# A two-branch layer on one core: merged table products, three more kinds of buffers, fewer idle products and a new written-out order

## The chip, the cores and the metric

The kernel runs on one core of a Trainium2 chip. A core has five engines that this document names as the profile does: PE (matrix products, with PEld for its weight loads), DVE (vector), ACT (scalar, with activation functions), POOL and SP (which here only issues transfers). The metric is the device time of one execution in microseconds (us).

## The reference

The input x has 2048 tokens of 512 channels. It is normalised (mean and variance over the channels), and two branches of the normalised xn are added to x:

```python
xn = _layernorm(x)
# A: a long convolution along the tokens, one kernel of 2048 lags per channel
P = exp(dt * A * l)                         # 512 channels x 128 complex modes x 2048 lags
K = real(sum over modes of C * P * dt * B)  # 512 x 2048
yA = irfft(rfft(xn, 4096) * rfft(K, 4096))[:2048] + xn * Dskip
# B: a gated unit
yB = (sigmoid(xn @ w_gate) * (xn @ w_up)) @ w_down    # 512 -> 1792 -> 512
out = x + yA + yB
```

Inputs and output are bf16.

## The kernel before

**Branch B** works in four groups of 512 tokens. For a group it takes the 1792 inner channels as 14 tiles of 128, two tiles at a time: a gate projection (four products of 128x512 into one PSUM bank, L1082), a sigmoid on ACT (L1098), an up projection (four products, L1107) and a product h on DVE (L1129). The table `UPS` gives each of the 28 pairs of tiles a mode: whether ACT first copies the up projection from PSUM to SBUF (L1118) and whether DVE multiplies both tiles in one instruction. In modes 2 and 3 DVE reads a wide SBUF copy, in 4 and 5 one half of it comes from PSUM, in 6 two SBUF halves, in 0 two PSUM halves, in 1 one wide PSUM operand. `GATES` lists pairs whose two sigmoids are one instruction. Then four down projections follow for the group, 14 products each (L1160).

**Branch A** replaces the Fourier transform of 4096 by two stages of products with small constant matrices. Stage one (L710, eight steps `fx2`) transforms xn along 32 rows; its result goes to DRAM (`z_scr`) and is loaded again in another layout. For each of two channel halves there are eight units, worked on two at a time, so eight pairs in all. For each pair come the forward product of the pair (L914, `fm`), the spectrum of the kernel from the lag table kT with a constant block E that is loaded for each unit (L930, `fk`), and the complex products of both on DVE (L935, L939). The inverse product of the pair follows (`mv_`). It exists in three forms, chosen by the table `SUMS`: with 0 the products go to PE as they are (L963); with 1 DVE first adds them once (L946, L947, `fsum`) and PE has fewer columns to stream (L975); with 2 DVE adds twice (L949 too) and PE has fewer still. The result goes to DRAM (`v_scr`) and comes back for the last stage (L1039, `s2_mm`), which is added to branch B's output: for the first three token groups by DVE (L1053) into a buffer, for the last group in PSUM, with DVE adding x at the end (L1180).

**The lag table.** K is built from powers of exp(dt A). A chain of 12 squarings in f32 (ACT L682, DVE L691 and L693) gives the powers W, which POOL casts to bf16 by a transfer (L687). From W the tables G and H are built for each of four channel chunks by complex products on DVE (`cmul`): two products of all of `lo` with the real and with the imaginary part of a power (L748, L749) and then a difference and a sum (L753, L754). There are ten such products in each chunk, with n = 1, 1, 2, 2, 4, 4, 4, 4, 7 and 8; one product has 256 n elements in each partition. PE contracts G and H over the modes (L833, `f_k`), a selection follows (L862), and kT is complete.

**What sets the order.** Every step is entered in a list (`pl.add`) with an engine and its dependences, and numbered in the order of entry. The list `ORDER` gives the sequence in which steps are issued; each engine works through its own steps in that sequence, waiting where a dependence is not met. SP's transfers are such a queue too: a transfer that waits holds up those behind it. Buffers come from pools of slots (`es` for E, `kb` for the kernel's spectrum, `vs` for results on their way to `v_scr`, `zx` for what comes back from `z_scr`); a slot is taken by `acq` and given back by `rel` as `ORDER` is read. `ON_DVE` lists, by number, copies and normalisations that go to DVE and not to ACT; `ON_ACT` lists the token tiles whose mean and variance ACT computes (L556 to L558) and not DVE (L561, L565, L566). Before the first data have arrived PE runs idle products of zeros (L541, `keep_warm`): one step of 9, and four steps whose lengths are in `WARM`.

Of the kernel before, what the change touches and what calls it, by code (L numbers as in the profile page):

```python
# [11 lines left out]
F32 = mybir.dt.float32  # L12
# [37 lines left out]
SUMS = ((0, 0, 0, 2), (1, 0, 1, 2))  # L50
WARM = (2, 2, 2, 2)
# [132 lines left out]
def _consts():  # L184
# [26 lines left out]
ORDER = [  # L211
# [131 lines left out]
def kernel(  # L343
# [83 lines left out]
    s1, mn = (at(OFF["pq"], [2, 64])[:, n, :] for n in range(2))  # L427
    s2 = at(OFF["tmp"], [2, 64])
    rr = at(OFF["tmp"] + KB // 2, [D])
    W = [at(OFF["W%d" % p], [12, 2, DW]) for p in range(NP)]  # L430
    gc = at(OFF["gc"], [2, D])
    xn = at(OFF["xn"], [NT, D])

# [245 lines left out]
    for k in range(12):  # L679
# [5 lines left out]
        def f_cw(cur=cur, k=k):  # L685
            for p in range(NP):
                P.dma_start(out=W[p][:, k], in_=cur[:, p])  # L687
# [570 lines left out]
```

## Time and profile before

| | |
|---|---|
| three runs | 213.96, 215.98 and 218.8 us; median 215.98 us |
| the profiled execution | 214.29 us, span 212.6 us |
| busy, share of the span | PE 202.3 us (95%), DVE 194.7 us (92%), ACT 171.3 us (81%), POOL 31.7 us (15%) |
| busy time of weight loads | 104.2 us (49%) |
| granted clock of PE | 0.999 |
| transfers | 42.37 MB, mean 199 GB/s |

The span goes from the first to the last instruction of the profiled execution. A row of the groups gives line, engine, operation, output and inputs with partitions x elements, the count, then busy time and the mean duration of one in ns, and then the engine's idle time just before such instructions with what ended it. "Big" is the name of the one large SBUF tile in which most buffers lie, "banks" is PSUM.

### The profile page before, as it was taken

The numbers are of one execution on the slowest core, as the hardware profiler recorded it, in microseconds if no ns is written. First come the engines' busy times: TensorE is split into PE (matmuls) and PEld (weight loads), VectorE is DVE, ScalarE is ACT, GpSimd is POOL, SyncE is SP. The second block draws the span as 40 slices with busy tenths as digits, with TensorE's granted clock in tenths as the row PEclk, the third lists the DMA queues.
The fourth block names the chain that finished last, engine by engine and source line by source line (L and its number), as shares of the span: only waits on it lengthen the run. The fifth ranks groups of instructions, "written<-read, shape, count | busy, mean of one in ns | idle before, by whom it ended". The sixth has DMA issues, their size and how long they took to land.

```text
span 212.6 us, 5668 instructions
## 1 busy us (share of the span) xinstructions
PE 202.3 (95%) x2263; PEld 104.2 (49%) x2291; DVE 194.7 (92%) x410; ACT 171.3 (81%) x272; POOL 31.7 (15%) x67
## 2 busy tenths in 40 slices
PE   7899999999999999999999999999999998999990
PEld 2664444444444354445556365446446554544570
DVE  3899999999999999999999999999999999892792
ACT  3899999999999997868989999949388997971000
POOL 4302316343240000004400000000010060000000
PEclk9999999999999999999999999999999999999999
DMA  6999999958976072594885333425765599989956
GB/s 193 380 417 366 311 243 215 199 112 192 193 129 171 18 233 100 152 266 130 150 263 165 108 92 100 142 99 166 213 204 105 171 294 221 338 241 267 204 186 224
DMA packets 44045, 42.37 MB, mean 199 GB/s; under 512 B 8809, under 2 KB 37746, under 8 KB 44018
## 3 DMA queue, kind: packets, MB, share of 16 engines
q1 hardware_dynamic: 39074, 36.95, 55.8%
q0 software_dynamic: 4512, 4.73, 14.2%
q8 instruction: 18, 0.29, 0.6%
q10 hardware_dynamic: 432, 0.33, 0.5%
q14 instruction: 9, 0.07, 0.1%
HBM read 25.21 MB, written 12.07 MB: 175 GB/s over the span
## 4 chain that ended last, share of the span: by engine, by line
PE 77%; ACT 13%; DMA 3%; DVE 2%; issue 2%; POOL 0%; SPq 0%; DVEq 0%; ACTq 0%; POOLq 0%
PE banks L1160 21%; PE banks L1107 17%; PE banks L1082 17%; PE banks L930 7%; ACT hT_sb L1098 3%; DMA v_scr<-big 3%; PE banks L541 3%; PE banks L833 3%; PE banks L963 2%; PE banks L914 2%; ACT big L297 2%; PE banks L862 1%; ACT big L682 1%; PE banks L975 1%; PE banks L710 1%
## 5 line engine op out<-in xcount | busy, mean ns | idle before, releaser
L297 ACT ACTIVATE big<-banks 128x1024 bf16<-128x1024 f32 (+4 forms) x78 | 71.2, 957 | 6.5 <-PE banks L963 2.2
L1082 PE MATMUL banks<-xnT,wg_sb 128*128 128x512 bf16 (+1 forms) x233 | 53.0, 361 | 1.2 <-ACT xnT L297 0.6
L1107 PE MATMUL banks<-xnT,wu_sb 128*128 128x512 bf16 x212 | 52.7, 380 | 0.8 <-issue 0.3
L1160 PE MATMUL banks<-wd_sb,hT_sb 128*128 128x512 bf16 (+1 forms) x233 | 50.1, 366 | 0.3 <-issue 0.2
L1160 PEld LDWEIGHTS <-hT_sb 128*128 128x128 bf16 x238 | 22.8, 98 | 25.2 <-issue 1.2
L1098 ACT ACTIVATE hT_sb<-banks 128x512 bf16<-128x512 f32 x56 | 32.4, 630 | 3.3 <-PE banks L1082 2.9
L1082 PEld LDWEIGHTS <-wg_sb 128*128 128x128 bf16 x244 | 22.8, 98 | 24.7 <-issue 3.9
L1107 PEld LDWEIGHTS <-wu_sb 128*128 128x128 bf16 x224 | 20.9, 98 | 25.6 <-issue 2.8
L748 DVE TENSOR_TENSOR big<-big 128x1024 bf16<-128x1024 bf16 (+4 forms) x40 | 26.8, 671 | 0.4
L749 DVE TENSOR_TENSOR big<-big 128x1024 bf16<-128x1024 bf16 (+4 forms) x40 | 26.7, 667 | 0.0
L1118 ACT ACTIVATE big<-banks 128x512 bf16<-128x512 f32 (+1 forms) x39 | 25.2, 677 | 0.6 <-PE banks L1107 0.5
L935 DVE TENSOR_TENSOR big<-big 128x2048 bf16<-128x2048 bf16 x16 | 19.4, 1222 | 1.0 <-ACT big L297 1.0
L930 PE MATMUL banks<-big 128*128 128x256 bf16 x160 | 20.1, 273 | 0.0
L930 PEld LDWEIGHTS <-big 128*128 128x128 bf16 x160 | 15.3, 98 | 5.4 <-issue 1.2
L802 ACT ACTIVATE sq_sb<-big 128x256 bf16<-128x256 bf16 (+2 forms) x20 | 13.4, 688 | 5.3 <-DVE big L754 4.1
L687 POOL DMA_DIRECT2D big<-big x24 | 13.0, 546 | 28.7 <-DVE big L693 19.7
L753 DVE TENSOR_TENSOR big<-big 128x512 bf16<-128x512 bf16 (+4 forms) x40 | 16.7, 417 | 0.2
L754 DVE TENSOR_TENSOR big<-big 128x512 bf16<-128x512 bf16 (+4 forms) x40 | 16.6, 415 | 0.0
L1129 DVE TENSOR_TENSOR hT_sb<-hT_sb,big 128x1024 bf16<-128x1024 bf16 (+1 forms) x29 | 16.0, 559 | 0.3 <-ACT big L1118 0.2
L682 ACT ACTIVATE big<-big 128x1024 f32<-128x1024 f32 x11 | 11.8, 1076 | 0.1
L561 DVE BATCH_NORM_STATS2 stats<-big 128x6 f32<-128x512 bf16 x12 | 8.3, 688 | 3.4 <-DMA big<-in_A_u_dram 3.4
L939 DVE TENSOR_TENSOR big<-big 128x1024 bf16<-128x1024 bf16 x16 | 11.0, 688 | 0.0
(101 smaller groups left out, 208.0 us busy)
## 6 DMA issues: line engine op xcount, KB each, us to landing
big<-c_E SPq DMA_DIRECT2D x16, 320.0 KB, 4.0
z_scr<-big SPq DMA_DIRECT2D x16, 256.0 KB, 2.8
big<-z_scr SPq DMA_DIRECT2D x16, 256.0 KB, 4.2
v_scr<-big SPq DMA_DIRECT2D x16, 256.0 KB, 3.3
big<-big POOLq DMA_DIRECT2D x24, 128.0 KB, 3.5
big<-in_A_u_dram SPq DMA_DIRECT2D x4, 512.0 KB, 7.8
big<-v_scr SPq DMA_DIRECT2D x4, 512.0 KB, 6.3
wu_sb<-in_B_w_up_dram SPq DMA_DIRECT2D x2, 896.0 KB, 10.4
```

The lines of the kernel that those rows point to most:

```text
L297: nc.scalar.activation(out=a, in_=b, func=ACT.Identity)
L748: V.tensor_tensor(out=wide(outp), in0=wide(lo), in1=mre, op=ALU.mult)
L749: V.tensor_tensor(out=wide(tb()), in0=wide(lo), in1=mim, op=ALU.mult)
L753: V.tensor_tensor(out=outp[:, :, 0], in0=outp[:, :, 0], in1=tb()[:, :, 1], op=opr)
L754: V.tensor_tensor(out=outp[:, :, 1], in0=outp[:, :, 1], in1=tb()[:, :, 0], op=opi)
L930: T.matmul(bank(sk[kt == NKT - 1])[:, DW * c:DW * c + DW], es()[:, c, kt, :], kT[p][:, kt, :], start=kt in (0, NKT - 1), stop=kt >= NKT - 2)
L935: V.tensor_tensor(out=pp()[:, :, 0:4, :], in0=xx()[:, :, 0, :].unsqueeze(2).to_broadcast([128, 2, 4, DW]), in1=kb().unsqueeze(1).to_broadc ...
L1082: T.matmul(bank(sl)[:, c0:c1], w_at(w, CUT_G, kt, k), xnT[:, grp, kt, c0:c1], start=(kt == 0), stop=(kt == KT - 1))
L1098: S.activation(out=o_, in_=i_, func=ACT.Sigmoid)
L1107: T.matmul(bank(sl), w_at(wu_sb, CUT_U, kt, k), xnT[:, grp, kt, :], start=(kt == 0), stop=(kt == KT - 1))
L1118: S.activation(out=o_, in_=i_, func=ACT.Identity)
L1160: T.matmul(bank(po)[:, 0:c[1] - c[0]], hT_sb[:, hts[k // 2].idx, k % 2, jj * 128:(jj + 1) * 128], wd_sb[:, k, c[0]:c[1]], start=first and ...
```

## The change

- In `cmul` the two products with the real and the imaginary part become one of twice the size where both results fit the temporary buffer of 2048 elements (n = 1, 2 and 4); the difference and the sum then read both from there. For this W is kept with real and imaginary part of a chunk side by side, the f32 powers too, and the first power is made by one product instead of two.
- `es` has six slots where it had three, `kb` three where it had two, `vs` three where it had two. The added ones lie in places that are free only later: those of `es` and `kb` after the lag tables are done, that of `vs` after the first forward product.
- `keep_warm` runs 8 idle products in its first step instead of 9, and 0, 2, 0, 2 in the others instead of 2, 2, 2, 2.
- For token tiles 4 to 15 epsilon is added to the variances once for four tiles and no longer once for each tile.
- `SUMS`, `UPS`, `GATES`, `ON_DVE` and `ON_ACT` have new entries. In `SUMS`, by the diff, the entry 0 stands twice (before: four times), 1 twice (twice) and 2 four times (twice).
- `ORDER` is a new list. The added epsilon steps move the numbers of later steps by up to three. Some numbers, before and after: the last stage-one product 154 and 132; the first forward product 338 and 341, with its two loads from `z_scr` 336, 337 and 340, 339; the second forward product 360 and 363; the last inverse product 507 and 510; the last two stores to `v_scr` 509, 511 and 512, 514. In the new list, on SP, 131 is the load that transposes the last token group, 350 the first load of E, and 169, 134, 171 and 136 are the last stores to `z_scr`.

```diff
-SUMS = ((0, 0, 0, 2), (1, 0, 1, 2))
-WARM = (2, 2, 2, 2)
+SUMS = ((0, 1, 0, 2), (1, 2, 2, 2))
+WARM = (0, 2, 0, 2)
...
-UPS = (5, 3, 5, 0, 3, 5, 2, 2, 1, 3, 5, 2, 2, 3, 3, 5, 2, 6, 2, 6, 3, 6, 2, 5, 2, 4, 2, 4)
-GATES = ()
-ON_DVE = (41, 99, 100, 101, 102, 111, 112, 126, 180, 181, 263, 293, 422, 442, 785, 787, 795)
-ON_ACT = (3, 7, 13, 15)
+UPS = (4, 5, 0, 0, 3, 3, 1, 2, 6, 2, 2, 5, 4, 5, 6, 2, 2, 2, 2, 6, 6, 3, 4, 2, 0, 2, 5, 0)
+GATES = (2, 6, 25)
+ON_DVE = (100, 101, 103, 115, 127, 183, 184, 214)
+ON_ACT = (2, 7, 8, 9, 14)
 ORDER = [
...
+    237, 238, 239, 233, 213, 167, 168, 698, 130, 240, 241, 131, 707, 242, 245, 169, 256, 234, 243, 246, 244, 170, 247,
+    132, 133, 257, 135, 709, 747, 350, 248, 258, 249, 251, 775, 259, 710, 737, 777, 708, 134, 776, 749, 264, 250, 265,
+    260, 267, 268, 732, 781, 171, 252, 266, 261, 269, 727, 270, 728, 296, 262, 739, 734, 748, 783, 253, 779, 136, 729,
+    272, 730, 271, 409, 273, 340, 276, 339, 341, 343, 263, 277, 778, 254, 344, 349, 342, 351, 361, 362, 735, 736, 751,
+    278, 365, 274, 780, 279, 345, 346, 275, 352, 347, 807, 785, 750, 363, 753, 809, 372, 808, 364, 366, 384, 373, 280,
...
+    491, 831, 822, 833, 859, 858, 832, 842, 844, 509, 490, 824, 860, 835, 501, 502, 470, 510, 492, 527, 826, 701, 865,
+    846, 872, 834, 836, 511, 512, 513, 514, 530, 531, 874, 876, 862, 864, 528, 855, 856, 866, 880, 883, 712, 802, 524,
+    702, 878, 881, 713, 612, 803, 804, 884, 525, 792, 613, 703, 893, 882, 521, 887, 805, 522, 714, 622, 793, 794, 704,
...
-    W = [at(OFF["W%d" % p], [12, 2, DW]) for p in range(NP)]
+    W = [at(OFF["W%d" % p], [12, 2, 2, CW]) for p in range(NP)]
...
-    warm = [keep_warm(9, -10)]
+    warm = [keep_warm(8, -10)]
...
+        if i1 > LN_ACT:
+            st = [pl.add("DVE", 0.08, lambda: V.tensor_scalar(out=ln_ve[:, i0:i1], in0=mv[:, i0:i1, 1], scalar1=EPS, scalar2=None, op0=ALU.add), st, prio)]
...
     def f_w0():
-        wd = lambda n: pt_[n].rearrange("p (w d) -> p w d", w=NP)
-        V.tensor_tensor(out=wt[0][:, :, 0], in0=wd("rr"), in1=wd("sh"), op=ALU.mult)
-        V.tensor_tensor(out=wt[0][:, :, 1], in0=wd("rr"), in1=wd("sn"), op=ALU.mult)
+        cs = at(pt0_sh, [2, D], F32).rearrange("p c (w d) -> p w c d", w=2 * NP)
+        V.tensor_tensor(out=wt[0], in0=pt_["rr"].rearrange("p (w d) -> p w d", w=2 * NP).unsqueeze(2).to_broadcast([128, 2 * NP, 2, CW]), in1=cs, op=ALU.mult)
...
     def cmul(lo, outp, n, m, conj, buf, deps, prio):
...
+        fit = 2 * ne <= 2048
+        flat = lambda v: v.rearrange("p r c k h -> p (r c) (k h)")
...
         def f_a():
-            V.tensor_tensor(out=wide(outp), in0=wide(lo), in1=mre, op=ALU.mult)
-            V.tensor_tensor(out=wide(tb()), in0=wide(lo), in1=mim, op=ALU.mult)
+            if fit:
+                V.tensor_tensor(out=tb()[:, 0:2 * ne], in0=flat(lo).unsqueeze(1).to_broadcast([128, 2, 2 * NPR, 2 * n]),
+                                in1=m.rearrange("p m (r h) -> p (m r) h", h=2).unsqueeze(2).to_broadcast([128, 2 * NPR, 2 * n, 2]), op=ALU.mult)
+                return
+            for i, o_ in enumerate((flat(outp), tb()[:, 0:ne])):
+                V.tensor_tensor(out=o_, in0=flat(lo), in1=m[:, i, :].rearrange("p (r h) -> p r h", h=2).unsqueeze(2).to_broadcast([128, NPR, 2 * n, 2]), op=ALU.mult)
...
-    kgen[3][0].rel += tuple(_Slot(k, i) for k, n, m in (("pp", 2, 3), ("zx", 2, 10)) for i in range(n, m))
+    kgen[3][0].rel += tuple(_Slot(k, i) for k, n, m in (("pp", 2, 3), ("zx", 2, 10), ("es", 3, 6)) for i in range(n, m))
+    kq_free[0].rel += (_Slot("kb", 2),)
...
-                es=[OFF["W0"], OFF["W0"] + 2560, OFF["W0"] + 5120], kb=[OFF["W0"] + 7680, OFF["W0"] + 9728],
-                vs=[OFF["xn"] + 14 * KB, OFF["lad"] + 10 * KB],
+                es=[OFF["W0"], OFF["W0"] + 2560, OFF["W0"] + 5120, OFF["lad"] + 12 * KB, OFF["tmp"] + 3 * KB // 2, None],
+                kb=[OFF["W0"] + 7680, OFF["W0"] + 9728, KQ], vs=[OFF["xn"] + 14 * KB, OFF["lad"] + 10 * KB, OFF["kx"] + 6 * KB],
...
+        if not v_st[0]:
+            mm.rel += (_Slot("vs", 2),)
```

More of the change, by code (lines that the diff above doesn't have):

```diff
@@ L557, in fa1 @@
                     S.activation(out=glu_sb[:, 7, :], in_=xn[:, i, :], func=ACT.Square, scale=-1.0, bias=mv[:, i, 0:1], accum_out=mv[:, i, 1:2])
-                    S.activation(out=ln_ve[:, i:i + 1], in_=mv[:, i, 1:2], func=ACT.Identity, scale=1.0 / D, bias=eps[:])
+                    if i < LN_ACT:
+                        S.activation(out=ln_ve[:, i:i + 1], in_=mv[:, i, 1:2], func=ACT.Identity, scale=1.0 / D, bias=eps[:])
+                    else:
+                        S.activation(out=mv[:, i, 1:2], in_=mv[:, i, 1:2], func=ACT.Identity, scale=1.0 / D)
             else:
@@ L565, in fa2 @@
                     V.bn_aggr(out=mv[:, i, :], in_=stats[:, i % 4, :])
-                    V.tensor_scalar(out=ln_ve[:, i:i + 1], in0=mv[:, i, 1:2], scalar1=EPS, scalar2=None, op0=ALU.add)
+                    if i < LN_ACT:
+                        V.tensor_scalar(out=ln_ve[:, i:i + 1], in0=mv[:, i, 1:2], scalar1=EPS, scalar2=None, op0=ALU.add)
             if i < LN_ACT:
@@ L618, in ptile @@
         return t
-    names = ["dtb", "z_re", "z_im", "w0", "rn", "rr", "sn", "sh"]
+    names = ["dtb", "z_re", "z_im", "w0", "rn", "rr", "sh", "sn"]
     pt_ = {n: ptile(BF if n == "dtb" else F32) for n in names}
+    pt0_sh = pt0[0] - 4 * KB
     pt0[0] = OFF["lad"] + 12 * KB
@@ L686, in f_cw @@
             for p in range(NP):
-                P.dma_start(out=W[p][:, k], in_=cur[:, p])
+                P.dma_start(out=W[p][:, k], in_=cur[:, 2 * p:2 * p + 2])
         c_op = pl.add("POOL", 1.0, f_cw, [cur_op], PLAD + k * 0.01 + 0.005, dma=(512 * KB, _rate(1024), 1.0))
@@ L774 @@
             for q in range(0, n, st):
-                last = cmul(G[:, :, :, q:q + st, :], G[:, :, :, n + q:n + q + st, :], st, W[c // 2][:, 4 + lev, :, ws],
+                last = cmul(G[:, :, :, q:q + st, :], G[:, :, :, n + q:n + q + st, :], st, W[c // 2][:, 4 + lev, c % 2],
                             True, "tg", [last, W_op[4 + lev]], PC)
@@ L896, in slot, with view @@
         sl = _Slot(pool)
-        return sl, lambda: at(HOME[pool][sl.idx], shape)
+        def view():
+            off = HOME[pool][sl.idx]
+            if off is not None:
+                return at(off, shape)
+            v = sq_sb[:].rearrange("p a b -> p (a b)")[:, 0:int(np.prod(shape))]
+            return v.rearrange("p (a b c) -> p a b c", a=shape[0], b=shape[1])
+        return sl, view
     v_st, z_free = [[] for _ in VPART], []
```

21 lines of the change are left out of this document (10 added, 11 removed), and 69 rows, old and new, of the table ORDER.

## The prediction

> **What bounds the kernel now.** I read the page's busy shares first, then the busy time of each engine in stretches, then the chain of waits.
>
> ```profile
> PE 202.3 (95%) x2263; PEld 104.2 (49%) x2291; DVE 194.7 (92%) x410; ACT 171.3 (81%) x272; POOL 31.7 (15%) x67
> ```
> ```profile
> 15.00:190.00 175.00, 171.96 (x2058) 86.52 (x2081) 171.96 (x363) 158.25 (x252) 27.27 (x49) 1.00 0.69 186
> ```
>
> The second row is the stretch from 15 to 190 us: 175 us, then the busy time of PE, of PE's weight loads, of DVE, ACT and POOL, and the granted clock, 1.00. PE and DVE are both busy for 171.96 us of it, 98%; ACT for 90%. So two engines bind at once, with 3.0 us idle each, and a change has to shorten both queues to move the end. That PE's busy time is real work shows in the chain of waits (start, us, what):
>
> ```profile
> 1.38 5.73 PE banks L541 x13
> ...
> 84.14 0.35 PE banks L710 x8
> 84.49 0.79 PE banks L862 x64
> ...
> 89.76 6.04 PE banks L1160 x28
> ...
> 96.59 1.42 PE banks L833 x123
> ...
> 126.30 1.44 PE banks L963 x64
> ...
> 183.61 0.79 PE banks L975 x32
> ...
> 189.69 0.57 PE banks L975 x16
> ```
>
> The 28 down products take 6.04 us, 0.216 us each with nothing between them; a group of four (one gate or up projection) is then 0.86 us and a group of 14 is 3.02.
>
> The Trainium skill, Perfetto Trace Analysis, Identifying the Most-Contended Engine, says that matmul busy time is a bad measure and weight-load share a better one. By that page PE, with 49% of weight loads, would have room and DVE alone would bind; the 0.216 us spacing of the 28 speaks against it. What would follow is the first rival.
>
> The profiled execution took 214.29 us, 1.7 over its span of 212.6. The three runs go from 213.96 to 218.8 with a median of 215.98, 0.8% above the profiled one. I sum against the span and scale at the end.
>
> **PE's part.** An inverse product of a pair costs 1.44 us without sums (L963), 0.79 after one step, 0.57 after two (both L975). By the diff two pairs leave the first kind, one to 0.79 and one to 0.57, and one goes from 0.79 to 0.57: 2.88 - 0.79 - 0.57 + 0.22 = 1.74 us less. The diff's table shows four pairs with two steps, not five; I cost four. Five idle products go: one of the 13 at the start (5.73 / 13 = 0.44 us each) and the two later pairs, of which the rows show the second:
>
> ```profile
> 28.62 0.60 PE L541 MATMUL banks<-glu_sb 128*128 128x512 bf16 x2
> ```
>
> At 0.216 us each these four are 0.86 us, in a queue with no room. PE: 1.74 + 0.86 + 0.44 = 3.0 us less. The first transposes stand right behind the idle products, so nothing takes that place.
>
> **DVE's part.** Groups, with busy time, then mean ns of one:
>
> ```profile
> L748 DVE TENSOR_TENSOR big<-big 128x256 bf16<-128x256 bf16 x8 | 3.0, 380 | 0.0
> L748 DVE TENSOR_TENSOR big<-big 128x512 bf16<-128x512 bf16 x8 | 3.5, 436 | 0.1
> L748 DVE TENSOR_TENSOR big<-big 128x1024 bf16<-128x1024 bf16 x16 | 11.1, 691 | 0.3
> L748 DVE TENSOR_TENSOR big<-big 128x2048 bf16<-128x2048 bf16 x4 | 4.9, 1222 | 0.0
> L946 DVE TENSOR_TENSOR big<-big 128x768 bf16<-128x768 bf16 x8 | 4.4, 553 | 0.0
> L949 DVE TENSOR_TENSOR big<-big 128x512 bf16<-128x512 bf16 x4 | 1.7, 425 | 0.1
> L561 DVE BATCH_NORM_STATS2 stats<-big 128x6 f32<-128x512 bf16 x12 | 8.3, 688 | 3.4 <-DMA big<-in_A_u_dram 3.4
> L566 DVE TENSOR_SCALAR ln_ve<-mv 128x1 f32<-128x1 f32 x12 | 1.8, 154 | 0.4
> L582 DVE TENSOR_SCALAR big<-big,mv,ln_ri 128x512 bf16<-128x512 bf16 x11 | 4.3, 414 | 0.2 <-POOL ln_ri L516 0.2
> L292 DVE CAST big<-banks 128x1024 bf16<-128x1024 f32 x2 | 2.4, 1220 | 0.0
> L292 DVE CAST big<-banks 128x512 bf16<-128x512 f32 x3 | 2.0, 691 | 0.0
> L1129 DVE TENSOR_TENSOR hT_sb<-hT_sb,big 128x1024 bf16<-128x1024 bf16 x15 | 10.2, 688 | 0.0
> L1129 DVE TENSOR_TENSOR hT_sb<-hT_sb,banks 128x512 bf16<-128x512 bf16 x10 | 6.7, 682 | 0.4 <-PE banks L1107 0.4
> L1129 DVE TENSOR_TENSOR hT_sb<-hT_sb,big 128x512 bf16<-128x512 bf16 x14 | 5.8, 420 | 0.3 <-ACT big L1118 0.2
> ```
> ```profile
> 168.23 0.55 DVE L946 TENSOR_TENSOR big<-big 128x768 bf16<-128x768 bf16 x1
> 168.70 0.55 DVE L947 TENSOR_TENSOR big<-big 128x768 bf16<-128x768 bf16 x1
> ```
>
> Neighbours overlap: the second row starts 0.47 us after the first, which lasts 0.55. So an instruction occupies DVE for its duration less 0.08 us.
>
> - **Merged products**, two of a size (L748 and its twin L749) into one of twice the size: 8 x (2 x 0.30 - 0.36) + 8 x (2 x 0.36 - 0.61) + 16 x (2 x 0.61 - 1.14) = 1.9 + 0.9 + 1.3 = 4.1 us less. The smallest kind costs more per element than the others; if its merged form keeps that, its 1.9 is nothing and the term is 2.2.
> - **Layernorm**: one statistics tile goes to ACT (0.61 and its aggregate 0.1), six 128x1 additions go (0.07 each): 1.2 less. Two normalisations go to ACT: 0.7 less.
> - **Copies**: ten on DVE become three. Two of 1.14, three of 0.61 and two small ones at about 0.35 go: 4.8 less.
> - **Sums**: four units more get a first step (two of 0.47) and four more a second (0.34): 5.1 more.
> - **GLU products**: counting the table of modes, 15 wide ones (0.61) become 12, 8 half-and-half (0.34 + 0.60) become 7, 3 of two SBUF halves (0.68) become 4, 1 of two PSUM halves (1.20) becomes 4: 1.5 more.
>
> DVE: -4.1 - 1.2 - 0.7 - 4.8 + 5.1 + 1.5 = -4.2 us. ACT takes what DVE gives away, 6.7 us at DVE's own durations: with it 158.25 becomes 165 of 175, 94%, still the third. The wide layout of W and the single product at w0 move the same elements; I cost them at nothing, hidden by the table chain's own waits on DVE. More buffers for E, kb and vs take away waits of ACT; one of those stopped PE, and I let it pay for waits that the new order brings:
>
> ```profile
> 180.07 0.62 PE L914 MATMUL banks<-big,m 64*32 64x512 bf16 x15 [0.96 <-ACT big L297]
> ```
>
> **The order, and the tail.** In the new list one up group more (0.86 us) stands behind the last inverse product, and seven h products of DVE in place of four (1.8 us). Ahead of that product PE thus has 3.9 us less and DVE 6.0 less. PE gives the smaller: 189.69 - 3.9 = 185.8 us. Behind it lie now:
>
> ```profile
> 191.41 1.34 SPq L448 DMA_DIRECT2D v_scr<-big  x2
> 192.80 4.83 SPq L448 DMA_DIRECT2D big<-v_scr  x7
> ```
> ```profile
> L448 SPq DMA_DIRECT2D big<-v_scr x5: 302/415/421, 195.5 to 197.2; - x5
> ...
> DMA to landing us min/median/max: 5.8/6.2/6.6
> ```
> ```profile
> 201.75 1.93 PE L1039 MATMUL banks<-big 128*64 128x256 bf16 x26
> ...
> 205.81 1.70 PE L1160 MATMUL banks<-wd_sb,hT_sb 128*128 128x256 bf16 x14
> ```
>
> The product ends at 190.26; ACT copies, SP has stored by 192.75, and only when that has landed, at 195.5, do the last loads leave; they land 5.8 to 6.2 us later, at 201.3 to 201.7. The product that needs them runs at 201.75: 11.5 us of other PE work covered a chain of 11.0 to 11.4. In the new list the cover is two up groups (1.72), two down groups (6.04) and three output products (4 matmuls each; the 26 above in 1.9 us make that 0.25): 8.5 us. If the chain stays at 11.4, PE waits 2.9 us; if the loads take 3 us, as the store did, the chain is 8.2 and PE waits for nothing. I take 1.5, the middle, because in the new list fewer large loads leave just ahead of the last.
>
> The Trainium skill, DMA: Bandwidth & Descriptors, section on queues, rings and completion order, says that an engine consumes descriptors in ring order, so a load waits for bytes issued ahead of it. By it the loads above were slow because of the large ones just ahead, and the wait would be near 0: 1.5 us less than my sum. No row of before has a last load alone.
>
> PE's end: before, 189.69 to 207.51 is 17.8 us; now 17.8 + 0.86 + 1.5 after 185.8 gives 206.0. From PE's end to the span's end were 5.1 us, of which 0.4 because the last addition stood behind others; the new list puts only its own two there: 4.7. Span 206.0 + 4.7 = 210.7, execution 212.4, 0.9% less; on the median 215.98 x 212.4 / 214.29 = 214.0.
>
> **Rivals.** *DVE alone sets the pace and the tail doesn't wait.* The last inverse product then comes 6.0 earlier, at 183.7; with 18.7 behind it and 4.7 at the end the span is 207.1, the execution 208.8, on the median 210.4. For it: an engine that idles 3.0 us has some to give. Against it: PE would have to give 2.1 of the 3.0. It is also what the Trainium skill's page on trace analysis, above, would have.
>
> *Loads come late (slower).* Forward products wait for a store and load through z_scr:
>
> ```profile
> 91.50 0.37 SPq L448 DMA_DIRECT2D big<-z_scr  x1
> ...
> 92.47 0.43 SPq L448 DMA_DIRECT2D big<-z_scr  x1
> ...
> 103.05 0.91 SPq L448 DMA_DIRECT2D big<-z_scr  x2
> ```
> ```profile
> 102.36 0.62 PE L914 MATMUL banks<-big,m 64*32 64x512 bf16 x16
> ...
> 110.37 0.62 PE L914 MATMUL banks<-big,m 64*32 64x512 bf16 x16
> ```
> ```profile
> DMA to landing us min/median/max: 2.4/3.8/6.2
> ```
>
> The last row counts stores and loads of z_scr alike. From the end of the last first-stage product (84.49) to the second load's landing (92.47 + 3.8 = 96.3) the chain took 11.8 us, up to 14.2 with the slowest landing; PE used it at 102.36. In the new list the PE work between is one down group (3.02), eight groups of four (6.9), one pair of table products (1.5) and one selection (0.8): 12.2 us. The slack of 6 us falls to 0.4, and three z stores now stand on SP behind a transposing load and an E load that wait themselves. For the second pair the cover falls from 7.4 us to 4.7, against 0.9 of issuing and 3.8 to 6.2 of landing. At 1 us for each of the eight pairs 8 us are lost: span 218.7, execution 220.4, on the median 222. It decides from 1.9 us of such waits on (my gain gone) and past 6.2 is slower by 2%.
>
> *The merged products fall to half rate.* A 2048 product at the 1.22 us that 1024 take from PSUM would be near 2.4; 32 of them add some 20 us. The innermost steps stay what they were, so it is unlikely: 235 us.
>
> **Numbers.** Forecast 0.57, DVE alone 0.20, late loads 0.20 (0.12 past 2%), half rate 0.03. About 2% is what this kernel's runs, spread over 2.2%, can tell from no change: 211.7 and 220.3. Faster 0.24 (0.19 of the first rival and 0.05 of the forecast, whose own range is 211 to 216), slower 0.15, within 2% 0.61. The range 209.8 to 219.5 takes in the first rival, the terms' bounds (1.9 for the merged products, 0 to 2.9 in the tail) and the milder half of late loads.
>
> **What would show it.** L748 with 512, 1024 and 2048 elements at 0.44, 0.69 and 1.22 us; DVE near 190.5 us busy, PE near 199; the last L975 of two steps near 185.8; PE idle before an L1039 near 194; the first L914 at 100 to 102 us with little idle before it. Waits of PE before L914 on z loads, or DVE idle for over 5 us between 15 and 185, would prove me wrong, as would a last inverse product before 184.

## The result, and the profile after

The changed kernel takes 222.88 us (median of four runs, 222.62 to 224.03), the kernel before 216.82 (213.96 to 218.8) beside it: a ratio of 1.041, with a 95% interval from 1.035 to 1.046. It is slower by 4%, where "within 2%" was forecast, and outside the range of 209.8 to 219.5. Some runs of a kernel are over 1.5% longer than its fastest; the ratios here leave these out, while the medians count every run, so a ratio isn't the quotient of two medians. The profiled execution took 222.68 us, 1.8 over its span of 220.9.

On the page of the changed kernel, its busy shares and then the engines' shares of the chain of waits:

```profile
PE 202.4 (92%) x2163; PEld 103.8 (47%) x2190; DVE 191.8 (87%) x375; ACT 175.1 (79%) x280; POOL 31.8 (14%) x67
...
DVE 29%; ACT 24%; PE 20%; DMA 19%; issue 5%; POOL 1%; SPq 0%; DVEq 0%; ACTq 0%
```

DVE's busy time fell by 2.9 us (forecast: by 4.2, to 190.5), but the span grew by 8.3. Before, the chain lay on PE for 77%; now it wanders over three engines and the transfers, so that each waits for another in turn. The busy time by stretches says where (stretch, length, then busy time of PE, its weight loads, DVE, ACT and POOL, and the granted clock), first of before, then of after:

```profile
33.80:46.00 12.20, 11.93 (x67) 5.38 (x69) 12.06 (x32) 12.13 (x23) 4.49 (x8) 1.00 0.89 192
75.00:112.00 37.00, 36.38 (x534) 18.61 (x526) 36.47 (x83) 31.04 (x55) 5.21 (x12) 1.00 0.65 180
```
```profile
15.00:190.00 175.00, 164.85 (x1897) 83.45 (x1918) 159.93 (x316) 155.39 (x250) 27.51 (x49) 0.99 0.66 175
...
33.80:46.00 12.20, 8.27 (x37) 3.19 (x37) 9.16 (x22) 6.24 (x13) 5.73 (x8) 0.86 0.77 130
...
75.00:112.00 37.00, 33.24 (x516) 16.18 (x522) 32.18 (x68) 31.38 (x58) 4.23 (x11) 1.00 0.53 150
```

In the whole stretch that the prediction used PE now idles for 10.1 us where it idled for 3.0, and DVE for 15.1. Of PE's 7.1 us more, 3.7 lie at 34 to 46 us and 3.1 at 75 to 112. The first place stands in the chain of waits (start, us, what):

```profile
24.50 6.20 DMA x_scr<-big
30.72 7.12 DMA xnT<-x_scr
37.88 1.16 PE banks L1105 x4
39.04 1.71 PE banks L1130 x4
40.75 3.74 PE banks L1183 x14
44.49 0.40 PE banks L717 x8
44.91 1.94 ACT big L298 x2
...
47.34 0.95 ACT big L689
```

Token group 1 can't start before its normalised rows have been stored to DRAM (`x_scr`) and loaded back transposed (L1105 is the old L1082; line numbers of after are 7 to 23 higher). PE has used up group 0 at 33.95 and stands still until 37.88, and 22 products then take 6.54 us (37.88 to 44.42) that at 0.216 each are 4.75: 1.8 us more, at a lower clock. ACT, whose next step is a copy of what PE produces behind those 22 (L717, the old L710), waits 4.8 us, and the squaring for W (L689, the old L682) stands behind that copy. So the table chain starts late, and DVE idles.

### The profile page after: what moved, and what is told of

Its sections match the earlier page's. It is cut to its first block, busy times and chain, and to the rows that moved or that the text cites. A ratio compares the mean times of both kernels' runs of the same rounds, so it can differ in the third digit from the quotient of the medians.

```text
span 220.9 us, 5436 instructions
## 1 busy us (share of the span) xinstructions
PE 202.4 (92%) x2163; PEld 103.8 (47%) x2190; DVE 191.8 (87%) x375; ACT 175.1 (79%) x280; POOL 31.8 (14%) x67
## 4 chain that ended last, share of the span: by engine, by line
DVE 29%; ACT 24%; PE 20%; DMA 19%; issue 5%; POOL 1%; SPq 0%; DVEq 0%; ACTq 0%
DVE big L755 9%; ACT big L298 8%; PE banks L1183 6%; DMA v_scr<-big 6%; DMA big<-big 5%; DVE big L759 4%; PE banks L1105 4%; DVE big L765 4%; PE banks L1130 4%; DVE big L766 4%; DMA xnT<-x_scr 3%; ACT hT_sb L1121 3%; ACT big L296 3%; DMA x_scr<-big 3%; PE banks L953 3%
## 5 line engine op out<-in xcount | busy, mean ns | idle before, releaser
L298 ACT ACTIVATE big<-banks 128x1024 bf16<-128x1024 f32 (+3 forms) x82 | 74.4, 959 | 10.7 <-PE banks L717 4.8
L1105 PE MATMUL banks<-xnT,wg_sb 128*128 128x512 bf16 (+1 forms) x233 | 53.4, 362 | 6.3 <-DMA xnT<-x_scr 3.9
L1105 PEld LDWEIGHTS <-wg_sb 128*128 128x128 bf16 x244 | 22.9, 97 | 31.0 <-issue 5.6
L1121 ACT ACTIVATE hT_sb<-banks 128x512 bf16<-128x512 f32 (+1 forms) x53 | 32.9, 654 | 0.0
L755 DVE TENSOR_TENSOR big<-big 128x2048 bf16<-128x2048 bf16 (+2 forms) x32 | 29.9, 939 | 2.7 <-ACT big L296 2.3
L1141 ACT ACTIVATE big<-banks 128x512 bf16<-128x512 f32 (+1 forms) x36 | 23.3, 664 | 0.0
L958 DVE TENSOR_TENSOR big<-big 128x2048 bf16<-128x2048 bf16 x16 | 19.4, 1219 | 1.4 <-PE banks L998 1.0
L759 DVE TENSOR_TENSOR big<-big 128x1792 bf16<-128x1792 bf16 (+1 forms) x16 | 17.8, 1151 | 2.7 <-ACT big L296 2.7
L953 PE MATMUL banks<-big 128*128 128x256 bf16 x150 | 18.0, 273 | 0.1
L953 PEld LDWEIGHTS <-big 128*128 128x128 bf16 x150 | 14.5, 98 | 3.8 <-issue 0.7
L1152 DVE TENSOR_TENSOR hT_sb<-hT_sb,big 128x512 bf16<-128x512 bf16 (+1 forms) x27 | 14.3, 535 | 0.6 <-ACT big L1141 0.6
L689 ACT ACTIVATE big<-big 128x1024 f32<-128x1024 f32 x11 | 12.0, 1088 | 1.1 <-DVE big L700 1.1
L1152 DVE TENSOR_TENSOR hT_sb<-hT_sb,banks 128x512 bf16<-128x512 bf16 (+1 forms) x16 | 11.3, 713 | 0.4 <-PE banks L1130 0.2
L793 POOL MEMSET big<- 128x128 bf16 x4 | 0.9, 218 | 73.8 <-DVE big L755 43.6
```

The lines of the kernel that those rows point to most:

```text
L298: nc.scalar.activation(out=a, in_=b, func=ACT.Identity)
L755: V.tensor_tensor(out=tb()[:, 0:2 * ne], in0=flat(lo).unsqueeze(1).to_broadcast([128, 2, 2 * NPR, 2 * n]), in1=m.rearrange("p m (r h) -> p ...
L759: V.tensor_tensor(out=o_, in0=flat(lo), in1=m[:, i, :].rearrange("p (r h) -> p r h", h=2).unsqueeze(2).to_broadcast([128, NPR, 2 * n, 2]), ...
L953: T.matmul(bank(sk[kt == NKT - 1])[:, DW * c:DW * c + DW], es()[:, c, kt, :], kT[p][:, kt, :], start=kt in (0, NKT - 1), stop=kt >= NKT - 2)
L1105: T.matmul(bank(sl)[:, c0:c1], w_at(w, CUT_G, kt, k), xnT[:, grp, kt, c0:c1], start=(kt == 0), stop=(kt == KT - 1))
L1121: S.activation(out=o_, in_=i_, func=ACT.Sigmoid)
```

## The experiments

The time of the kernel before went from 214.1 to 216.8 us between groups of runs, so ratios to the kernel before beside it are compared; the changed kernel's is 1.041. The expectations call PE by its name and DVE VectorE, ACT ScalarE, POOL GpSimd and SP SyncE. In kernels in which the list was written anew, line numbers are 9 lower than in the changed kernel, in those with a halved load 8 higher or, with both, 1 lower.

**Is it the edits or the order?** Four kernels have the old list and the old tables of copies. The first has all edits of the change:

```diff
 # the changed kernel with
-UPS, GATES, ON_DVE, ON_ACT, ORDER of the change
+those of before, renumbered; the three shared epsilon steps put in
```

> All edits of the change (merged products, more buffers, fewer idle matmuls, new sums, shared layernorm addition) run in the order and with the copy, gate and layernorm tables of the kernel before. Theory 'the new order loses the time' (first transposing load of x_scr late, PE idle 3.9 us, then a lower clock): none of that can happen here, the busy work is 2 to 3 us smaller than before, so the time is 0.5 to 2% under the kernel before, about 213 to 216. Rival 'the edits themselves cost it' (merged forms or the new homes of the buffers bring waits): the time is near the changed kernel's, 220 to 224.

Measured: 219.62 us, ratio 1.025 (1.017 to 1.034). So a good part of the loss comes without the new order and the first theory falls; but the time isn't near the changed kernel's either. Two waits stand out in its trace, one of DVE and one of PE (L989 is the inverse product of a pair, the old L975, and L963 the last step of the sums):

```profile
DVE ln_ve L569 <- ACT mv L553: 2.5, 1, 2.5
```
```profile
PE banks L989 <- DVE big L963: 3.1, 2, 2.7
```

The first is an artefact of where the shared epsilon step was put: DVE stood for a statistic of ACT. The second hangs on the new sums, in an order not made for them. Without them:

```diff
-SUMS = ((0, 1, 0, 2), (1, 2, 2, 2))
+SUMS = ((0, 0, 0, 2), (1, 0, 1, 2))
```

> As the run beside it, but the sums keep their old levels, so DVE does 5.1 us less of them and PE 1.7 us more by the prediction's sizes. If DVE binds in the old order, this is 1 to 3 us faster than with the new sums; if PE binds, it is 1 to 2 us slower. Theory 'the new order loses the time': 211 to 215, below the kernel before. Rival 'the edits themselves cost it': 219 to 223.

Measured: 216.79 us, 1.011 (1.004 to 1.018), between the ranges of the two theories. The new sums cost 2.8 us here; DVE's busy time differs by 5.2 us (197.0 and 191.8), so the term of 5.1 was right.

Then with the epsilon steps at a better place, directly ahead of POOL's power:

```diff
-    ..., last of four statistics, epsilon, ..., power, ...
+    ..., last of four statistics, ..., epsilon, power, ...
```

> All edits but the sums in the old order, as before, with the three shared layernorm additions put directly ahead of GpSimd's power in the order (they stood ahead of other work there and held VectorE for 2.5 us at 19 us). That wait goes: 1 to 1.5 us less than the run without it, 215 to 216, which is the time of the kernel before within 0.5%: VectorE does 3 us less, but PE, at 99%, sets the pace. Rival 'VectorE sets the pace': 212 to 213.5.

Measured: 216.87 us, 1.010 (1.005 to 1.015). Of DVE's wait 0.5 us are left, and the time is the same, so that wait was worth nothing that shows; 2.4 us less of work on DVE (192.3 for 194.7) bought nothing. PE waits 1.4 us for the first transposing load here. Last, the idle matmuls of before and sums for one pair more:

```diff
-SUMS = ((0, 0, 0, 2), (1, 0, 1, 2))
+SUMS = ((0, 1, 0, 2), (1, 0, 1, 2))
-WARM = (0, 2, 0, 2)       # and 8 in the first step
+WARM = (2, 2, 2, 2)       # and 9
```

> The order, tables and idle matmuls of the kernel before, with the merged products, the shared layernorm addition and the additional buffers, and one step of sums for one more pair (PE 0.65 us less, VectorE 0.94 us more). PE is at 99% there, so by its own theory (PE binds, VectorE's saving goes to waste) the time is 0 to 1.3 us under the kernel before. Rival 'both bind': 2 to 3 us under it, since VectorE does 2 us less and PE 0.65 us less.

Measured: 216.75 us, 1.006 (1.001 to 1.011). In the old order, then, what the edits save in busy time is no time. For the idle matmuls the reason shows in a run of their own:

```diff
 # the kernel before with
-WARM = (2, 2, 2, 2)
+WARM = (0, 2, 0, 2)
-    warm = [keep_warm(9, -10)]
+    warm = [keep_warm(8, -10)]
```

> The kernel before with only the five idle matmuls taken out (one of 13 at the start, the pairs at 17 and 28.6 us). The prediction's term: PE is 1.3 us shorter and the time 1.3 us (0.6%) less. Rival 'they filled waits': PE's idle time before 35 us grows by as much as they took, and the time is the same within 0.3%.

Measured: 217.43 us, 1.006 (0.9995 to 1.013): no gain. In its trace PE waits where it did not before (L1107 is the up projection):

```profile
PE banks L1107 <- DMA xnT<-x_scr: 0.8, 1, 0.8
```

The pair at 28.6 us stood where PE waits here for the same transposing load. In the first 40 us PE's busy time is 1.5 us less (36.2 for 37.7), so its idle time is 1.5 us more, and the expectation that they filled waits came true.

**What of the first wait costs the time?** Five kernels change what happens around 34 us. First the clock:

```diff
-WARM = (0, 2, 0, 2)
+WARM = (0, 2, 16, 2)      # and step 22 moved directly ahead of 667 in ORDER
```

> The changed kernel with 16 idle matmuls (3.4 us) ahead of the first gate of token group 1, where PE stands still for 3.9 us, so that PE stays busy and still reaches the gate when the load has landed. Theory 'the pause costs a second time by the clock that falls after it': the granted clock stays at 1.00 from 35 to 45 us, and the time is 2 to 2.5 us less, about 220.5. Rival 'the lower clock lies on no path': the clock stays at 1.00 and the time within 0.7 us of 222.9.

Measured: 223.59 us, 1.043 (1.036 to 1.049). The clock stays at 1.00, the first product with the tables (L845, the old L833) starts 1.1 us sooner (79.8 for 80.9), and nothing is left of it at the end: at the fourth of them PE is 0.6 us later (162.4 for 161.8). The load landed 0.75 us later here than in the changed kernel (at 38.6 us), and still PE was 0.95 us sooner with the eight products for which ACT waits (43.5 for 44.4). The lower clock alone isn't the loss; a PE that is earlier by itself didn't shorten this kernel.

Then the stores of W. POOL's queue in the new list issues step 3 of the ladder ahead of step 2, 8 ahead of 7 and 10 ahead of 9, and step 3's value isn't there until 29.9 us, so that two steps leave together. SP's and POOL's issues in before, then in after:

```profile
24.90 0.38 SPq L448 DMA_DIRECT2D x_scr<-big  x1
...
30.61 1.68 SPq L600 DMA_TRANSPOSE xnT<-x_scr  x1
```
```profile
26.96 1.04 POOL L687 DMA_DIRECT2D big<-big  x2 [3.18 <-DVE big L693]
32.23 1.04 POOL L687 DMA_DIRECT2D big<-big  x2 [4.22 <-DVE big L693]
```
```profile
30.22 2.09 POOL L694 DMA_DIRECT2D big<-big  x4 [6.82 <-DVE big L700]
```

```diff
 ORDER = [     # steps 2, 7 and 9 of the ladder ahead of 3, 8 and 10
-    ..., 69, ..., 66, ..., 84, 81, ..., 90, ..., 87, ...
+    ..., 66, 69, ..., 81, 84, ..., 87, 90, ...
```

> The changed kernel with the stores of W put in the sequence of the ladder on GpSimd's queue (step 2 ahead of 3, 7 ahead of 8, 9 ahead of 10; three entries of the order moved). Theory 'the two steps that leave GpSimd together at 30.2 us collide with the first transposing load': only one step leaves there, the load lands about 2 to 2.7 us sooner (4.4 to 5 us in place of 7.1), PE waits 1.2 to 2 us in place of 3.9, the clock falls less or not at all, and the time is 3 to 5 us less, 218 to 220. Rival 'the load is late for itself, PE only comes too soon': the wait stays 3.5 to 4 us and the time within 1 us of 222.9.

Measured: 220.84 us, 1.020 (1.006 to 1.035), an interval too wide to say by how much: the four runs go from 217.5 to 222.0 us, and the trace is of one of 221.7. In it the expected mechanism was half of the matter. The transposing load took 5.2 us in place of 7.1, but the store ahead of it 8.6 in place of 6.2, and PE still waited:

```profile
24.09 0.38 SPq L440 DMA_DIRECT2D x_scr<-big  x1
32.72 1.98 SPq L598 DMA_TRANSPOSE xnT<-x_scr  x1
```
```profile
PE banks L1096 <- DMA xnT<-x_scr: 4.4, 1, 4.4
```

So the collision with the load is real, and taking it away wasn't enough. Why the store was slow isn't shown: two steps of W left while it was under way, at 26.10 and 29.80 us, but in the kernel before one left 2 us behind the store too, and it took 5.7. What the store stands behind in any case is the load of w_down on its own queue, which landed at 29.4 us in the changed kernel:

```diff
 ORDER = [
-    ..., 13, 12, 16, 54, ..., 100, 104, 63, ...
+    ..., 13, 12, 54, ..., 100, 104, 16, 63, ...
```

> The changed kernel with one entry of its order moved: the load of w_down (1.8 MB) is issued on SyncE's queue behind the first x_scr store instead of ahead of it. Theory 'the first x_scr round trip starts the loss': the store, which left at 24.5 and landed only at 30.7 behind the large load, lands at 27 to 28, the transposing load by 33 to 35, PE waits 0 to 1 us in place of 3.9, the clock stays at 1.00, ScalarE isn't held for 4.8 us, and the time falls by 5 to 8 us to 215 to 218. Rival 'the later waits of the table chain (85 to 107 us) stand by themselves': the first wait goes, but the time falls by no more than 2 us, as when idle matmuls filled that wait.

Measured: 223.40 us, 1.038 (1.031 to 1.046). The store landed early (24.01 to 28.02), as expected; then the transposing load stood behind the 1.8 MB in its turn and took 11.2 us:

```profile
24.01 0.39 SPq L440 DMA_DIRECT2D x_scr<-big  x1
24.44 0.51 SPq L440 DMA_DIRECT2D wd_sb<-in_B_w_down_dram  x1
28.02 5.52 SPq L598 DMA_TRANSPOSE xnT<-x_scr  x1
```

PE waited 5.8 us, 1.9 longer than in the changed kernel, and the time is the same. The first wait didn't go, so this run tests neither theory. Next, ACT's wait without PE's:

```diff
 ORDER = [
-    ..., 173, 607, 147, 73, ...
+    ..., 173, 147, 607, 73, ...
```

> The changed kernel with one entry of its order moved: the 8 small products of the first stage (0.4 us) for which ScalarE waits 4.8 us until 44.9 us are issued ahead of the 14 down products (3 us, 3.9 at the low clock) in place of behind them. PE's work and its first wait stay as they are. Theory 'the pause reaches the end by ScalarE's queue and the ladder of W behind it, not by PE's own lost time': ScalarE's wait falls by 3 to 4 us, the last store of W leaves 3 to 4 us sooner (61.5 to 62.5 in place of 65.5), and the time falls by 2.5 to 4 us, to 219 to 220.5. Rival 'PE's lost time itself sets the end': the time stays within 0.7 us of 222.9.

Measured: 225.92 us, 1.050 (1.040 to 1.059). The ladder did end 2.7 us sooner (its last store left at 62.9, not 65.5; PE's first wait was 2.2 us here, not 3.9, though the edit doesn't touch it) and the first product with the tables came at 78.5, but by the second it stood at 104.3, behind the changed kernel's 103.7: PE waited 4.1 us for ACT at 90 to 100 us. My account of ACT's queue as the only path falls. By the idle matmuls and this run neither PE's time nor ACT's sets the end alone; what one engine gained by itself was given back further on. So the wait was taken from all of them at once:

```diff
-                def fg(k=k, sl=ga[e], w=wg_sb, grp=grp, c0=0, c1=512):
+                def fg(k=k, sl=ga[e], w=wg_sb, grp=grp * (grp != 1), c0=0, c1=512):
...
-                def fu(k=k, sl=ub[e], grp=grp):
+                def fu(k=k, sl=ub[e], grp=grp * (grp != 1)):
```

> The changed kernel, in which the gate and up products of token group 1 read the transposed rows of group 0 (so the output is not the reference's); the transposing load runs as before, but nobody waits for it. PE's 3.9 us at 34 us and the lower clock behind it go, and ScalarE's 4.8 us behind them. Theory A 'the first x_scr round trip is the loss, with all that follows it': 6 to 7 us less, 215.5 to 217. Theory B 'three in-order queues without slack: the table chain between VectorE and ScalarE at 80 to 107 us sets the pace by itself, and a gain ahead of it is given back there': no more than 3 us less, 220 to 223.

Measured: 217.26 us, 1.014 (1.010 to 1.019). The wait, the clock and ACT's wait are gone together, and with them 5.6 us, about what PE lost by the pause and the clock (3.9 and 1.8) and a little short of the 6 to 7 expected: theory A holds for that much. The first place is as busy as before (PE 11.93, ACT 12.13 us there); the second is left as it was, against 36.38 us of before:

```profile
33.80:46.00 12.20, 12.05 (x75) 5.02 (x75) 12.19 (x31) 11.92 (x22) 5.73 (x8) 1.00 0.82 140
75.00:112.00 37.00, 33.38 (x547) 17.58 (x551) 32.28 (x67) 31.10 (x56) 4.24 (x11) 1.00 0.54 147
```

So theory B is right in this, that the waits at 75 to 112 us stand by themselves.

**The second place.** The changed kernel's trace, ACT and then DVE (L584 normalises, L296 copies seeds of the tables, and L759 is a product that needs them):

```profile
89.09 0.80 ACT L584 ACTIVATE big<-big,ln_nb,ln_ri 128x512 bf16<-128x512 bf16 x1
...
90.27 0.80 ACT L584 ACTIVATE big<-big,ln_nb,ln_ri 128x512 bf16<-128x512 bf16 x1
90.97 1.20 ACT L296 ACTIVATE big<-big 128x512 bf16<-128x512 bf16 x2
```
```profile
92.21 2.09 DVE L759 TENSOR_TENSOR big<-big 128x1792 bf16<-128x1792 bf16 x2 [2.18 <-ACT big L296]
```

Two normalisations, one of which was DVE's before (0.35 us there), stand on ACT ahead of the seeds for which DVE idles.

```diff
-ON_DVE = (100, 101, 103, 115, 127, 183, 184, 214)
+ON_DVE = (100, 101, 103, 113, 114, 115, 127, 128, 129, 183, 184, 214)
```

> The changed kernel with four normalisations of token groups 2 and 3 put on VectorE (0.35 us each) instead of ScalarE (0.85 us each), at their places in the order. Two of them stand on ScalarE's queue at 89 to 91 us ahead of the seed copies for which VectorE then waits 2.2 us. Theory B: that wait shrinks by about 1.6 us and the time falls by 1.5 to 3 us, to 220 to 221.5. Theory A: the time stays within 1 us of 222.9, because the stretch is only late by what came before.

Measured: 221.45 us, 1.034 (1.029 to 1.039), 1.4 us less. DVE's wait of 2.2 us is gone; a smaller one before another L759 is left. In all, in the changed kernel and then here:

```profile
DVE big L759 <- ACT big L296: 2.7, 2, 2.2
```
```profile
DVE big L759 <- ACT big L296: 0.5, 1, 0.5
```

That is what theory B expected, if at its lower end and with intervals that still meet.

Then the sums:

```diff
-SUMS = ((0, 1, 0, 2), (1, 2, 2, 2))
+SUMS = ((0, 0, 0, 2), (1, 0, 1, 2))
```

> The changed kernel with the levels of sums of the kernel before: VectorE does 5.1 us less and PE 1.7 us more, from 115 us on. If VectorE and its chain set the pace of the second half (theory B), 2 to 4 us less, 219 to 221; if PE does, 1 to 2 us more, 224 to 225.

Measured: 228.91 us, 1.066 (1.057 to 1.076): both expectations missed by far. DVE has 5.1 us less to do and waits more than that (L958 multiplies spectra, the old L935, and L986 is the inverse product without sums):

```profile
DVE big L958 <- ACT big L298: 7.4, 3, 4.3
DVE big L958 <- PE banks L986: 2.9, 2, 2.3
```

Three pairs' inverse products became longer, and DVE stands for what comes behind them. The new list was made with the new sums, as the old one with the old, so taking the sums out alone says nothing of what they are worth.

And the three edits (group 1 without its wait, the normalisations, the old sums) together:

> The three edits of the runs beside it in one kernel (the output is not the reference's, since group 1 reads group 0's rows). If the causes lie one after the other and add, the gains add: by theory B 5 to 9 us less in all, 214 to 218. If each only makes the next wait longer, no better than the best of the three by more than 1 us.

Measured: 220.71 us, 1.030 (1.025 to 1.036), 3.5 us more than with the first wait gone alone: the old sums spoil this one as well.

**Mending it, with the reference's output.** The load of w_down in two halves:

```diff
-    l_wd = load("SP", wd_sb[:], B_w_down.rearrange("(k p) d -> p k d", k=FT), 1792 * KB)
+    wd_v = B_w_down.rearrange("(k p) d -> p k d", k=FT)
+    l_wd = load("SP", wd_sb[:, 0:7], wd_v[:, 0:7], 896 * KB)
...
+            Y.dma_start(out=wd_sb[:, 7:14], in_=wd_v[:, 7:14])   # in step 18, behind the transposing load
```

> The changed kernel with the load of w_down in two halves: the first where the whole stood, the second on the same queue behind the first transposing load. Theory A: the x_scr store lands at about 28 to 28.5 us in place of 30.7, the transposing load by 33 to 34.5, PE waits 0 to 1 us for it, the clock stays at 1.00 and the time falls by 4.5 to 6 us, to 217 to 218.5, as in the run that read other rows. Rival 'the transposing load is slow in itself, by the stores of W that leave at 30.2 us': it still lands at 36 us or later, and no more than 2 us are gained.

Measured: 219.59 us, 1.023 (1.005 to 1.041). In the profiled execution the store landed 3.5 us after it left, the load took 5.9, and PE didn't wait for it. So theory A's mechanism came, while the 3.3 us gained are less than the 4.5 to 6 expected, and the interval is wide. With the normalisations on DVE as above:

> Both the halved load and the four normalisations on VectorE. If the two losses lie one after the other, their gains add: 1.2 to 1.8 us less than the halved load alone. If the second is only the echo of the first, the same time within 0.5 us.

Measured: 217.28 us, 1.010 (1.006 to 1.015), 2.3 us less, where 1.2 to 1.8 were expected if the gains add. The second loss isn't an echo of the first. In the profiled execution PE now waits 0.7 us for the transposing load and 1.8 for the second half of w_down, so the mend isn't free. With the stores of W in sequence as above:

> As the run beside it, with the stores of W in the sequence of the ladder on GpSimd's queue. VectorE waited 2 us for those stores and the ladder ended 7 us later than before; if the ladder still sets the table chain, 0.5 to 2 us less; if not, the same within 0.5 us, or up to 2 us more where a store of W now stands ahead of the x_scr store's bytes.

Measured: 215.63 us, 1.005 (1.000 to 1.010), some 1.6 us less again. The ladder's last store left only 0.5 us sooner (61.7 for 62.2); what is gone in the profiled execution are 2.9 us in which DVE waited for these stores and PE's waits of 0.7 and 1.8 us. With the store no longer behind the whole of w_down and the stores of W spaced, the round trip takes 8.7 us (25.22 to 33.9, where the changed kernel took 13.4), and nobody waits for it. SP's issues, and the transposing load's time to its landing:

```profile
25.22 0.38 SPq L440 DMA_DIRECT2D x_scr<-big  x1
28.61 2.04 SPq L606 DMA_TRANSPOSE xnT<-x_scr  x1
```
```profile
xnT<-x_scr SPq DMA_TRANSPOSE x1, 5.3
```

Last, three seed copies on DVE as well (225, 266 and 296 added to `ON_DVE`):

> The kernel with the halved load, the four normalisations on VectorE and the stores of W in sequence, and three seed copies of the tables (0.3 us each) on VectorE as well, two of them where the kernel before had them; VectorE waited 1.4 us for ScalarE ahead of one of them. If ScalarE's queue is what holds the table chain, 0.8 to 1.5 us less than without, about 214.2 to 214.9, some 0.5% under the kernel before. If the chain of squares and products is as long in itself, the same within 0.5 us.

Measured: 214.99 us, 1.003 (0.999 to 1.007). The expected 0.5% under the kernel before isn't there; it is level with it. The stretch that the prediction used:

```profile
15.00:190.00 175.00, 171.62 (x1975) 85.99 (x1981) 169.05 (x334) 157.06 (x250) 27.66 (x49) 1.00 0.70 186
```

PE's 10.1 us of idle time are 3.4 again. At 75 to 112 us PE is busy for 35.1 of the 36.4 us of before, so most of the second place is mended too. No version tried beats the kernel before.

## Why the prediction was wrong

**The step that failed** is in "The order, and the tail": "PE gives the smaller: 189.69 - 3.9 = 185.8 us". The last inverse product starts at 198.43. That step moved the end by work alone. For waits of the new list ahead of the tail it allowed only what the removed one of 0.96 us would pay for, and, as a rival, those for `z_scr`. In their place the runs showed three losses that it hadn't asked about.

- *The first x_scr round trip* (5.6 us by the run without it). It was to be had from the trace of before: the transposing load left at 30.61, took 4.4 us and so landed at 35.0, and PE used it at 36.14, a slack of 1.1 us. In the new list PE is through with group 0 at 33.95. That alone gives 1.1 us of waiting; the rest, 2.8 us, is that the load left 0.1 later and took 7.1 us, with two steps of W leaving from half a microsecond ahead of it on. The prediction looked at SP's queue for z and v, and neither at x nor at POOL's queue, where the list has three pairs of steps the wrong way round.
- *ACT's queue* (1.4 us by the normalisations, 2.3 with the load halved). "ACT takes what DVE gives away ... still the third": third it was (175.1 us, 79% of the span; 3.8 us more, for the 6.7 costed), but that didn't make it harmless. Which engine is third over the whole span says nothing of who stands ahead of whom in an in-order queue.
- *The ladder's stores out of sequence* (some 1.6 us in the kernel with the load halved and the normalisations moved; by the traces through DVE's wait for them and the transfers beside them, not through an earlier end of the ladder).

PE's first products on group 1's rows, in before and in after (in brackets the idle time ahead of them):

```profile
36.14 1.03 PE L1082 MATMUL banks<-xnT,wg_sb 128*128 128x512 bf16 x4
```
```profile
37.88 1.16 PE L1105 MATMUL banks<-xnT,wg_sb 128*128 128x512 bf16 x4 [3.93 <-DMA xnT<-x_scr]
```

**PE's term, -3.0 us, did not come.** PE is busy for 202.4 us where 199 were forecast; 1.8 of that is the lower clock. The inverse products shrank by 1.2 us, not 1.74. Before and after:

```profile
L963 PE MATMUL banks<-big 32*64 32x512 bf16 (+1 forms) x256 | 6.0, 324 | 0.0
...
L975 PE MATMUL banks<-big 32*64 32x512 bf16 (+1 forms) x96 | 3.3, 346 | 0.0
```
```profile
L998 PE MATMUL banks<-big 32*64 32x512 bf16 (+1 forms) x128 | 4.6, 356 | 0.0
...
L986 PE MATMUL banks<-big 32*64 32x256 bf16 (+1 forms) x128 | 3.5, 323 | 0.1
```

(L986 is L963 of before, without sums, and L998 is L975.) The two pairs left without sums take 1.75 us each, where four took 1.5. The 1.3 us of idle matmuls are no saving at all: "in a queue with no room" was false for them, since idle time took their place.

**DVE's term was -2.9 us for -4.2**: 191.8 us busy for the forecast 190.5. The merged products saved 2.7 us and not 4.1: the six kinds of before hold 35.1 us in 64 instructions, those of after 29.9 in 32, each less 0.08 us of overlap.

```profile
L755 DVE TENSOR_TENSOR big<-big 128x2048 bf16<-128x2048 bf16 x16 | 19.5, 1221 | 0.6 <-ACT big L296 0.3
...
L755 DVE TENSOR_TENSOR big<-big 128x1024 bf16<-128x1024 bf16 x8 | 5.7, 711 | 1.4 <-ACT big L296 1.4
L755 DVE TENSOR_TENSOR big<-big 128x512 bf16<-128x512 bf16 x8 | 4.7, 603 | 0.7 <-ACT big L296 0.6
```

2048 and 1024 elements came at 1.22 and 0.71, as predicted (1.22 and 0.69); the smallest came at 0.60, not 0.44, which saves 0.08 us each over two of 0.38, the overlap taken off. The bound of 2.2 held. "Half rate" is refuted by the same rows. In the old order the saving was worth nothing in time; in the new one no run takes the merged products out.

**The tail** went better than forecast. Behind the last inverse product PE ran on:

```profile
198.43 0.64 PE L998 MATMUL banks<-big 32*64 32x512 bf16 x16
199.00 1.90 PE L1130 MATMUL banks<-xnT,wu_sb 128*128 128x512 bf16 x8
200.74 6.21 PE L1183 MATMUL banks<-wd_sb,hT_sb 128*128 128x512 bf16 x27
206.88 2.17 PE L1062 MATMUL banks<-big 128*64 128x256 bf16 x30
```

No wait, where 1.5 us (0 to 2.9) were forecast. The sum by the rule of the Trainium skill, DMA: Bandwidth & Descriptors, section on queues, rings and completion order, which said near 0, was the better one. The first of the last loads left at 205.1 us and took 2.6, those behind it up to 5.5, where the last loads of before took 5.8 to 6.6; no run changes what stands ahead of them alone. PE's end to the span's end is 3.8 us, forecast 4.7.

Two slips in the prediction's sums change nothing: the layernorm's 0.61 + 0.1 + 6 x 0.07 is 1.1 us and not 1.2, and 4 of 26 output products in 1.93 us are 0.30 us and not 0.25.

**The rivals.** "Loads come late" forecast 222 us, and 222.9 was measured, but not by its mechanism: the first forward product came at 112.4 (forecast: 100 to 102), and PE didn't wait for z loads before it. The number was right by chance. It had the right kind of cause at the wrong round trip. "DVE alone sets the pace" is refuted: DVE idles for 15.1 us. The sign that the prediction named against itself, DVE idle for more than 5 us between 15 and 185, is the one that came.

Left open: with the three losses mended, the last inverse product of the last kernel still starts at 189.9 us, 4.1 later than forecast. PE idles for 3.4 us between 15 and 190 there, 0.7 of it for the transposing load; the inverse products fall short by 0.5 us and the idle matmuls by 1.3. What else there is of it wasn't measured by itself.

## What to carry to other kernels

When an order is replaced, list every round trip through DRAM and every transfer that an engine waits for, and compute for each its landing in the old trace, its first use in the old trace, and its first use in the new list; here a slack of 1.1 us was gone with the new list. Check each queue, also those of POOL and SP, for steps out of their sequence of readiness. Where three engines work in order and all are over 80% busy, busy time saved on one of them need not be time saved (here 2.4 us of DVE and 1.3 of PE were not). Price a wait by taking it from all engines at once, as in the run with group 0's rows, and ask of filler work whether a wait would stand in its place.

## What the runs showed of the hardware

**The clock falls after a pause of PE.** Behind the pause of 3.9 us, microsecond by microsecond (the third figure from the end of a row is the granted clock):

```profile
38.00:39.00 1.00, 1.00 (x5) 0.44 (x4) 1.00 (x3) 0.00 (x0) 0.00 (x0) 0.83 0.93 163
39.00:40.00 1.00, 1.00 (x4) 0.29 (x2) 1.00 (x6) 0.92 (x1) 0.66 (x2) 0.50 0.00 0
...
41.00:42.00 1.00, 1.00 (x4) 0.41 (x3) 1.00 (x3) 0.00 (x0) 0.55 (x1) 0.50 1.01 157
42.00:43.00 1.00, 1.00 (x6) 0.39 (x4) 0.99 (x5) 0.00 (x0) 0.71 (x2) 0.96 0.10 13
```

In the row left out it is 0.50 too. So it is half the clock for some 3.4 us, from some 0.8 us after PE has begun again, and 1.8 us of PE's time. The Trainium skill, TensorE: Matmul & The Clock Gate, section "What's actually happening", has the clock halved after an idle window of about 3.4 us and given back after as long a busy one; the trace agrees, with a pause of 3.9 us and 3.4 us at half clock. A pause of 2.2 us, in the kernel with the z products first, left the clock at 1.00.

**A transposing load of 512 KB takes longer beside other transfers.** The first one took 4.4 to 5.7 us in the six kernels with the old list, where one step of W leaves 1.1 to 2.5 us behind it (4.4 in the kernel before), and 6.5 to 7.8 in the seven with the new list and POOL's queue as it was, where two steps leave from 0.2 to 1.3 us ahead of it on (the kernel with w_down later and those with the load halved not counted). With POOL's queue alone put in sequence it was 5.2. It was 11.2 with 1.8 MB ahead on its own queue and two steps of W beside it. The Trainium skill, DMA: Bandwidth & Descriptors, section "Issuing engines are not separate DMA queues", says that the transfers of SP and POOL interleave on the same 16 engines; these durations agree with it.
